# First loads of a channel-gating kernel as whole tiles on alternate queues, in place of halves on both

## The chip, the core and the metric

One core of a Trainium2 chip runs the kernel; the other seven do nothing of it. Names used below: TensorE does matmuls, VectorE sums and multiplies, ScalarE and SyncE mainly issue transfers here; 16 DMA engines move the data between the chip's main memory and SBUF, the memory on the core. A transfer has landed when the last of its completion updates has come in. The metric is the device time of one execution in microseconds (us), lower is better. Kernels are compared only within the same rounds. A ratio is the mean time of one kernel's fast runs over that of the other's of the same rounds, so it is not quite the ratio of the medians that are quoted; it comes with a 95% interval, and anything within 2% is called the same. A run over 1.5% above the fastest of its kernel counts as slow, and slow runs are not compared.

## The reference, cut to what matters

```python
x: (1, 384, 384, 384) bf16      # 113.25 MB
w1d: (1,) bf16                  # k = 1
g = mean of x over H and W      # one value per channel
s = sigmoid(g * w1d[0])
out = x * s                     # broadcast over H and W
```

Every output needs the mean of the whole input, so read literally x would be read twice. The kernel avoids that: it guesses the gate from the first four rows of each partition, gates and stores with that guess while it also sums everything, and at the end compares the true gate with the guess, bit by bit in bf16. If they differ, a second pass redoes all.

## The kernel before

x is seen as 1152 rows of 384 channels on each of 128 partitions: one first tile of 12 rows ("base"), and 19 tiles of 60 rows that go through 4 slots of SBUF. A row is 768 B per partition, a 60-row tile 46080 B per partition and 5.898 MB in all.

SyncE and ScalarE each issue DMAs into a queue of their own (in the profile q1 is SyncE's and q10 ScalarE's). The first loads (comments added, other lines cut):

```python
FIRST, EARLY, TILE, SLOTS, BOTH, FORE, OWN = 12, 4, 60, 4, 3, 32, 16
...
LEAD = EARLY + 4
load(base, FIRST, 0, hi=LEAD)                        # 8 of the 12 rows, SyncE
plan.dma("sync", w_one[0:1, 0:1], w1d.unsqueeze(0), writes=["w_one"])
for k in range(SLOTS):                               # slots 0, 1, 2 in halves, slot 3 whole
    load(slot(k), TILE, row0(k), ("sync", "scalar") if k < BOTH else ("sync",))
    if k == 0:
        load(base, FIRST, 0, ("scalar",), lo=LEAD)   # the other 4 rows, ScalarE
```

Then, for each tile, VectorE sums 16 of the 60 rows (`sum_own`, 10.5 us), TensorE sums the other 44 by matmuls with ones, VectorE multiplies the tile by the gate in place (`gate`, 12.1 us), ScalarE issues the store, and SyncE's load of the tile four later waits until that store has landed. A short ScalarE instruction delays load 4 once (comment added, the end of the loop cut):

```python
for k in range(n_tiles):
    if k >= SLOTS:
        for i in range(2) if k == SLOTS else () if k < SLOTS + 2 else (k - SLOTS,):
            sum_own(i)
            put(slot(i), TILE, row0(i), parts=None if i else (FORE, TILE - FORE))
        if k == SLOTS:
            pause(slot(k))     # ScalarE, 3.08 us; it waits for store 0 to land
        load(slot(k), TILE, row0(k), reads=["pause"] if k == SLOTS else ())
```

`put` is the gating and the issue of the store.

Of the kernel before, what the change touches and what calls it, by code (L numbers as in the profile page):

```python
# [149 lines left out]
def split(n, most):  # L150
    k = -(-n // most)
    return [n // k + (i < n % k) for i in range(k)]
# [3 lines left out]



FIRST, EARLY, TILE, SLOTS, BOTH, FORE, OWN = 12, 4, 60, 4, 3, 32, 16


PAUSE = 9
# [2 lines left out]
def bass_standalone__channel_attn_eca__vision_kernel(  # L165
# [5 lines left out]
    B, H, W, C = x.shape  # L171
    assert B == 1 and C == ROW and (B * H * W) % (4 * P) == 0
    n_rows = B * H * W // P
    x_rows, o_rows = x.flatten_outer_dims(), out.flatten_outer_dims()

    def dram(view, r0, n):
        return view[r0 * P : (r0 + n) * P, :].rearrange("(p t) c -> p (t c)", p=P)
# [21 lines left out]
    def at(r0, n):  # L199
        assert r0 + n <= n_arena  # L200
        return arena[:, r0 * C : (r0 + n) * C]

    def rows(r0, n):
        return [("sb", r) for r in range(r0, r0 + n)]
# [7 lines left out]
    base = SLOTS * TILE  # L212
# [5 lines left out]
    def slot(k):  # L218
        return k % SLOTS * TILE

    def row0(k):
        return FIRST + k * TILE
# [2 lines left out]
    s_true = at(base + FIRST, 1)  # L225
    plan = Planner(nc, "a", 70)

    def load(place, n, r0, queues=("sync",), lo=0, hi=None, reads=()):

        i, hi = lo, hi or n  # L230
        for queue, m in zip(queues, split(hi - lo, -(-(hi - lo) // len(queues)))):
            plan.dma(
                queue,
                at(place + i, m),
                dram(x_rows, r0, n)[:, i * C : (i + m) * C],
                reads=reads,
                writes=rows(place + i, m),
            )
            i += m

    loaded = []

# [40 lines left out]
    def sum_others():  # L283

        def one(e, s):
            e.wait_ge(ready, 1).then_inc(ready, -1)  # L286
            for r, n in ((0, FORE), (FORE, TILE - OWN - FORE)):
                add_rows(e, 1, (slot(s) + r) * C, n, False, False).then_inc(
                    plan.sems["tensor"], 1
                )  # L290

        def emit(e):
            add_rows(e, 1, (base + EARLY) * C, 4, True, False)
            rounds = -(-n_tiles // SLOTS)
            some = n_tiles - (rounds - 1) * SLOTS
            with e.Fori(0, rounds) as k:
                for s in range(some):
                    one(e, s)
                if some < SLOTS:
                    with e.If(k < rounds - 1):  # L300
                        for s in range(some, SLOTS):
                            one(e, s)
            add_rows(
                e, 1, (base + EARLY + 4) * C, FIRST - EARLY - 4, False, True
            ).then_inc(plan.sems["tensor"], 1)

        plan.streams["tensor"].append(("block", emit, None))
# [16 lines left out]
    def sum_own(k):  # L324

        r0 = slot(k) + TILE - OWN
        view = at(r0, OWN).rearrange("p (t c) -> p c t", t=OWN)
        to = part if k else own
        plan.op(
            "vector",  # L330
            lambda e: e.reduce_sum(to[:], view, axis=mybir.AxisListType.X),  # L331
            reads=rows(r0, OWN),
            writes=["part" if k else "own"],
        )
        if k:
            plan.op(
                "vector",
                lambda e: e.tensor_tensor(own[:], own[:], part[:], ALU.add),  # L338
                reads=["own", "part"],
                writes=["own"],  # L340
            )
# [37 lines left out]
    def put(place, n, r0, to=None, parts=None):  # L379
        to, i = place if to is None else to, 0  # L380
        for m in parts or [n]:
            plan.op(
                "vector",
                gate(to + i, place + i, m, s_early),
                reads=["s_early"] + rows(place + i, m),
                writes=rows(to + i, m),
            )
            i += m
        plan.final.append(
            plan.dma("scalar", dram(o_rows, r0, n), at(to, n), reads=rows(to, n))  # L390
        )

    def pause(r0):

        to = at(base + FIRST + 1, PAUSE)
        plan.op(
            "scalar",
            lambda e: e.activation(  # L398
                to, warm[:, 0:1].broadcast_to([P, PAUSE * C]), ACT_F.Sigmoid
            ),  # L400
            reads=["warm"],
            writes=rows(r0, 1) + ["pause"],
        )
# [26 lines left out]

    plan.op("gpsimd", lambda e: e.memset(warm[:, 0:1], 0.0), writes=["warm"])
    plan.op("vector", lambda e: e.memset(ones[:], 1.0), writes=["ones"])  # L432
    LEAD = EARLY + 4
    load(base, FIRST, 0, hi=LEAD)
    plan.dma("sync", w_one[0:1, 0:1], w1d.unsqueeze(0), writes=["w_one"])
    for k in range(SLOTS):
        load(slot(k), TILE, row0(k), ("sync", "scalar") if k < BOTH else ("sync",))
        if k == 0:
            load(base, FIRST, 0, ("scalar",), lo=LEAD)
    heads = {e: len(plan.streams[e]) for e in ("sync", "scalar")}  # L440
    weight()
    sum_first()
# [6 lines left out]
        reads=["total", "w_scaled0", "warm1"],  # L449
        writes=["s_early"],  # L450
    )
    plan.need("tensor", rows(base, LEAD))
    sum_others()

    for k in range(n_tiles):
# [5 lines that stand above are left out]
            if k == SLOTS:  # L461
                pause(slot(k))
            load(slot(k), TILE, row0(k), reads=["pause"] if k == SLOTS else ())
        there = rows(slot(k), TILE) + (rows(base + LEAD, FIRST - LEAD) if k == 1 else [])
        plan.relay(ready, "gpsimd", "tensor", there, rows(slot(k), FORE), ["acc1"])
        plan.signals("tensor", rows(slot(k) + FORE, TILE - OWN - FORE), ["acc1"])
    plan.signals("tensor", rows(base, FIRST), ["acc1"])
    for k in range(n_tiles - SLOTS, last):
# [15 lines left out]
        reads=["total", "w_scaled1"],  # L484
        writes=["s_true"],
# [6 lines left out]
        reads=["s_true", "s_early"],  # L492
        writes=["total"],
# [4 lines left out]
        reads=["total"],  # L498
        writes=["wrong"],
# [4 lines left out]
        reads=["wrong"],  # L504
        writes=["redo"],
# [5 lines left out]
    half, r0 = base // 2, 0  # L511
    for k, n in enumerate(split(n_rows, half)):
        place = k % 2 * half
# [4 lines left out]
            reads=rows(place, n),  # L518
            writes=rows(place, n),
# [98 lines left out]
```

## Time and profile before

| | before |
|---|---|
| time, median of 3 | 528.53 us (527.85 to 528.61) |
| bytes through the DMA engines | 226.5 MB, 430 GB/s over the span |
| VectorE busy | 451.1 us, 86% |
| TensorE busy | 178.2 us, 34% |
| 12-row tile: 8 rows landed / 4 rows landed | 7.7 / 22.4 us |
| slot 0 landed (first half / second half) | 18.5 / 14.5 us |
| store 0, 1, 2 issued | 38.6, 61.7, 84.7 us |
| store 0 landed, load 4 issued | 74.2, 77.3 us |

The timeline of VectorE before (start, length in us, engine, line, operation, operands; in brackets the idle time ahead of it and what ended it):

```profile
108.36 10.55 DVE L331 TENSOR_REDUCE part<-arena 128x384 f32<-128x6144 bf16 x1 [0.73 <-DMA arena<-in_x_dram]
135.47 10.54 DVE L331 TENSOR_REDUCE part<-arena 128x384 f32<-128x6144 bf16 x1 [3.90 <-DMA arena<-in_x_dram]
```

From 14.6 us on VectorE never waits for a load until tile 4, at 108 us; from tile 5 on it waits about 4 us for each. So VectorE has spare time in most of the run and none in the first 108 us.

### The profile page before, as it was taken

The page shows a single profiled execution, that of the slowest core. Times are in us where ns is not written, and L with a number is a line of the kernel's source. Part 1 is how long each engine was busy: PE and PEld are TensorE (multiplying, and loading weights), DVE is VectorE, ACT ScalarE, POOL GpSimd, SP SyncE. Part 2 cuts the span into 40 slices and gives each one's busy share as a digit, 9 for nine tenths or more (in the row PEclk, how much of TensorE's full clock was granted, in tenths as well). Part 3 has the DMA queues.
Part 4 walks back from the last instruction along what each step waited for, and adds up shares of the span by engine and source line. Part 5 has one row for each costly group of instructions (what it writes and reads, how often), then busy time and mean ns, then how long its engine had stood idle before and what let it go on. Part 6 is the DMA issues. An engine that isn't in the chain of part 4 may idle for free.

```text
span 526.7 us, 905 instructions
## 1 busy us (share of the span) xinstructions
PE 178.2 (34%) x640; PEld 0.2 (0%) x2; DVE 451.1 (86%) x82; ACT 5.8 (1%) x5; POOL 0.3 (0%) x5
## 2 busy tenths in 40 slices
PE   2534660060606051414233241515060606060701
PEld 0000000000000000000000000000000000000000
DVE  1899999999796969796969696979697979889796
ACT  1000020000000000000000000000000000000000
POOL 0000000000000000000000000000000000000000
PEclk9978877576766767675858585858585858576765
DMA  9999999999999999999999999999999999999998
GB/s 387 430 422 460 406 448 395 444 448 448 395 444 448 448 395 444 448 441 402 444 448 434 409 445 444 434 413 441 448 430 416 441 444 434 416 441 444 430 420 367
DMA packets 6340, 226.51 MB, mean 430 GB/s; under 512 B 706, under 2 KB 706, under 8 KB 962
## 3 DMA queue, kind: packets, MB, share of 16 engines
q10 hardware_dynamic: 3456, 122.49, 53.8%
q1 hardware_dynamic: 2882, 104.01, 45.9%
q14 instruction: 2, 0.02, 0.0%
HBM read 113.25 MB, written 113.25 MB: 430 GB/s over the span
## 4 chain that ended last, share of the span: by engine, by line
DMA 64%; DVE 27%; issue 4%; PE 2%; ACT 0%; DVEq 0%
DMA out_dram<-arena 33%; DMA arena<-in_x_dram 31%; DVE arena L209 13%; DVE part L331 12%; PE acc L247 1%; DVE own L338 1%; DVE total L319 0%; DVE own L356 0%; DVE terms L349 0%; ACT arena L481 0%; DVE total L489 0%; DVE total L374 0%; DVE wrong L497 0%; PE acc_own L247 0%; DVE redo L503 0%
## 5 line engine op out<-in xcount | busy, mean ns | idle before, releaser
L247 PE MATMUL acc<-arena,ones 128*128 128x512 bf16 x635 | 176.3, 447 | 314.0 <-PEq L286 314.0
L209 DVE TENSOR_TENSOR arena<-arena,s_early 128x23040 bf16<-128x23040 bf16 (+3 forms) x21 | 233.5, 11123 | 5.2 <-DMA arena<-in_x_dram 4.0
L331 DVE TENSOR_REDUCE part<-arena 128x384 f32<-128x6144 bf16 x18 | 189.5, 10526 | 53.4 <-DMA arena<-in_x_dram 53.4
L331 DVE TENSOR_REDUCE own<-arena 128x384 f32<-128x6144 bf16 x1 | 10.5, 10495 | 1.1 <-DMA arena<-in_x_dram 1.1
L338 DVE TENSOR_TENSOR own<-own,part 128x384 f32<-128x384 f32 x18 | 10.0, 558 | 0.6
L247 PE MATMUL acc_own<-terms,ones 128*128 128x384 bf16 x3 | 1.4, 478 | 16.8 <-DVE terms L349 16.8
L424 DVE TENSOR_SCALAR w_scaled<-w_all 128x1 f32<-128x1 f32 x2 | 0.2, 152 | 7.9 <-PE w_all L415 7.9
L481 ACT ACTIVATE arena<-total,w_scaled 128x384 bf16<-128x384 f32 x1 | 0.6, 614 | 444.3 <-DVE total L319 444.3
L319 DVE TENSOR_TENSOR total<-total,acc 128x128 f32<-128x128 f32 (+2 forms) x11 | 4.5, 408 | 0.4
L398 ACT ACTIVATE arena<-warm 128x3456 bf16<-128x3456 f32 x1 | 3.1, 3082 | 60.1 <-DMA out_dram<-arena 60.1
L415 PE MATMUL w_all<-w_one,ones 1*128 1x1 bf16 x1 | 0.2, 159 | 9.2 <-DMA w_one<-in_w1d_dram 9.2
L317 DVE COPY total<-acc 128x384 f32<-128x384 f32 x1 | 0.6, 558 | 1.2 <-PE acc L247 1.2
L409 ACT ACT_TABLE_LOAD x1 | 1.3, 1283 | 2.8 <-issue 2.8
L432 DVE MEMSET ones<- 128x128 bf16 x1 | 0.2, 165 | 1.3 <-PEq L603 1.3
L356 DVE TENSOR_TENSOR own<-own,terms 128x384 f32<-128x384 f32 x2 | 1.1, 559 | 0.1
L489 DVE TENSOR_TENSOR total<-arena,s_early 128x384 f32<-128x384 uint16 x1 | 0.6, 559 | 0.7 <-ACT arena L481 0.7
L349 DVE CAST terms<-own 128x384 bf16<-128x384 f32 x3 | 1.1, 357 | 0.1
L374 DVE TENSOR_TENSOR total<-total,acc_own 128x384 f32<-128x384 f32 x1 | 0.6, 556 | 0.6 <-PE acc_own L247 0.6
L446 ACT ACTIVATE s_early<-total,w_scaled 128x384 bf16<-128x384 f32 x1 | 0.6, 614 | 9.2 <-DVE total L319 9.2
L245 PE MATMUL acc<-arena,ones 128*128 128x512 bf16 x1 | 0.6, 608 | 0.0
L497 DVE TENSOR_REDUCE wrong<-total 128x1 f32<-128x384 f32 x1 | 0.6, 553 | 0.0
L409 ACT ACTIVATE warm<-warm 128x1 f32<-128x1 f32 x1 | 0.2, 202 | 0.0
(8 smaller groups left out, 0.9 us busy)
## 6 DMA issues: line engine op xcount, KB each, us to landing
out_dram<-arena ACTq DMA_DIRECT2D x19, 5760.0 KB, 44.7
arena<-in_x_dram SPq DMA_DIRECT2D x16, 5760.0 KB, 40.9
arena<-in_x_dram ACTq DMA_DIRECT2D x3, 2880.0 KB, 34.5
arena<-in_x_dram SPq DMA_DIRECT2D x3, 2880.0 KB, 29.0
out_dram<-arena ACTq DMA_DIRECT2D x1, 1152.0 KB, 11.1
arena<-in_x_dram SPq DMA_DIRECT2D x1, 768.0 KB, 7.7
arena<-in_x_dram ACTq DMA_DIRECT2D x1, 384.0 KB, 21.2
w_one<-in_w1d_dram SPq DMA_DIRECT2D x1, 0.0 KB
```

Source lines behind the costliest of these rows:

```text
L209: return lambda e: e.tensor_tensor(to_v, v, s_b, ALU.mult)
L245: loaded.append(e.matmul(bank, weights, moving, start=start, stop=stop))
L247: return e.add_instruction(mybir.InstMatmult(name=nc.get_next_instruction_name(), engine=mybir.EngineType.PE, ins=[e.lower_ap(moving), e.l ...
L317: emit = lambda e, part=part, of=of: e.tensor_copy(part, of)
L319: emit = lambda e, part=part, of=of: e.tensor_tensor(part, part, of, ALU.add)
L331: lambda e: e.reduce_sum(to[:], view, axis=mybir.AxisListType.X),
L338: lambda e: e.tensor_tensor(own[:], own[:], part[:], ALU.add),
L349: lambda e, term=term: e.tensor_copy(term, own[:]),
L356: lambda e, term=term: e.tensor_tensor(own[:], own[:], term, ALU.subtract),
L374: lambda e: e.tensor_tensor(total[:], total[:], acc_own[:, :C], ALU.add),
L398: lambda e: e.activation(to, warm[:, 0:1].broadcast_to([P, PAUSE * C]), ACT_F.Sigmoid),
L409: lambda e: e.activation(warm[:, 1:2], warm[:, 0:1], ACT_F.Sigmoid),
```

## The change

The intent is simpler loads: no tile is cut, both queues fed with long packets. SyncE's queue takes base, slot 1 and slot 3; ScalarE's takes slot 0 and slot 2.

```diff
-    LEAD = EARLY + 4
-    load(base, FIRST, 0, hi=LEAD)
+    load(base, FIRST, 0)
     plan.dma("sync", w_one[0:1, 0:1], w1d.unsqueeze(0), writes=["w_one"])
     for k in range(SLOTS):
-        load(slot(k), TILE, row0(k), ("sync", "scalar") if k < BOTH else ("sync",))
-        if k == 0:
-            load(base, FIRST, 0, ("scalar",), lo=LEAD)
+        load(slot(k), TILE, row0(k), "sync" if k % 2 else "scalar")
 ...
-    plan.need("tensor", rows(base, LEAD))
+    plan.need("tensor", rows(base, FIRST))
 ...
-        there = rows(slot(k), TILE) + (rows(base + LEAD, FIRST - LEAD) if k == 1 else [])
+        there = rows(slot(k), TILE)
```

(The body of `load`, which now issues one DMA, is cut.)

More of the change, by code (lines that the diff above doesn't have):

```diff
@@ L155 @@
 WIDE = 512
-FIRST, EARLY, TILE, SLOTS, BOTH, FORE, OWN = 12, 4, 60, 4, 3, 32, 16
+FIRST, EARLY, TILE, SLOTS, FORE, OWN = 12, 4, 60, 4, 32, 16
 PAUSE = 9
@@ L226, in bass_standalone__channel_attn_eca__vision_kernel, with load @@
     plan = Planner(nc, "a", 70)
-    def load(place, n, r0, queues=("sync",), lo=0, hi=None, reads=()):
-        i, hi = lo, hi or n
-        for queue, m in zip(queues, split(hi - lo, -(-(hi - lo) // len(queues)))):
-            plan.dma(
-                queue,
-                at(place + i, m),
-                dram(x_rows, r0, n)[:, i * C : (i + m) * C],
-                reads=reads,
-                writes=rows(place + i, m),
-            )
-            i += m
+    def load(place, n, r0, queue="sync", reads=()):
+        plan.dma(
+            queue, at(place, n), dram(x_rows, r0, n), reads=reads, writes=rows(place, n)
+        )
     loaded = []
```

## The prediction

> **What bounds the kernel now.** I read the page first (shares, slices, bytes), then a table of busy times by stage, then the issues and landings of single transfers, and last the first 110 us of the timeline. From the page:
>
> ```profile
> span 526.7 us, 905 instructions
> ...
> DMA  9999999999999999999999999999999999999998
> ...
> HBM read 113.25 MB, written 113.25 MB: 430 GB/s over the span
> ```
>
> The reader is to see that no slice has idle DMA engines: 226.5 MB go through them, and nothing in the change alters a byte of that. By stage (columns: stretch and length in us, busy us of PE, PEld, DVE, ACT, POOL, clock, DMA share, GB/s):
>
> ```profile
> 2.00:14.50 12.50, 2.83 (x7) 0.20 (x2) 2.76 (x8) 2.10 (x3) 0.00 (x0) 1.00 1.02 433
> 14.50:38.60 24.10, 11.83 (x39) 0.00 (x0) 22.79 (x4) 0.00 (x0) 0.00 (x0) 0.89 1.00 429
> 38.60:74.20 35.60, 19.32 (x69) 0.00 (x0) 35.53 (x6) 0.00 (x0) 0.00 (x0) 0.79 1.03 435
> 74.20:108.30 34.10, 5.70 (x26) 0.00 (x0) 33.39 (x4) 3.08 (x1) 0.00 (x0) 0.65 1.00 432
> 108.30:271.80 163.50, 54.41 (x198) 0.00 (x0) 139.07 (x18) 0.00 (x0) 0.00 (x0) 0.69 1.00 433
> 271.80:490.00 218.20, 72.80 (x264) 0.00 (x0) 185.45 (x25) 0.00 (x0) 0.00 (x0) 0.69 1.00 434
> ```
>
> From 2 us to 490 us the transfers run at 429 to 435 GB/s, whether only loads are under way (the first two rows) or loads and stores, and whether VectorE (DVE) is nearly always busy (the third and fourth rows) or 85% busy. So the DMA engines are the bound, VectorE is close behind only up to 108 us, and at 433 GB/s the 226.5 MB alone take 523 us of the 526.7. All that a change of queues could save is the rest, about 4 us or 0.7%; what it could cost is any stretch in which both queues are empty.
>
> **What the Trainium skill says.** "DMA: Bandwidth & Descriptors", Specifications, gives a fabric ceiling of 435 GB/s; the trace agrees (432 to 434 in the long stages). The same page, "Issuing engines are not separate DMA queues", says that the queues of SyncE and ScalarE run on the same 16 engines, and that a second issuer saves only issue time. The trace agrees in the last stage: the stores that ScalarE alone has in flight land at 496.7, 510.3 and 523.9 us (issue plus issue-to-landing of each), 5.898 MB every 13.6 us, 434 GB/s from one queue. Its section "Queues, rings and completion order" says that each engine round-robins between its queues packet by packet. That matters here, because a queue with short packets then gets a small share of the bytes. The DMA view of the stretch from 14.5 to 22.4 us, when ScalarE's queue holds the last four rows of the first tile (3072 B on each partition) and SyncE's holds half tiles (23040 B):
>
> ```profile
> DMA packets 289, 3.41 MB, mean 431 GB/s; under 512 B 32, under 2 KB 32, under 8 KB 158
> ...
> q1 hardware_dynamic: 143, 2.93, 86.1%
> q10 hardware_dynamic: 146, 0.48, 14.9%
> ```
>
> Equal packets (143 and 146), bytes of 6 to 1. So a packet is one partition's run, and each engine has 8 of them per transfer. At 433/16 = 27.1 GB/s per engine one takes 0.23 us (8 rows), 0.34 us (12 rows), 0.85 us (30 rows), 1.70 us (60 rows). The check: 8 rounds of 0.85 + 0.11 us are 7.7 us, and those four rows landed at 22.4 us, 7.9 us after the transfer ahead of them (14.5).
>
> **The change, part by part.** (1) It removes four of eight first loads and their issues: 3 halves and the four-row piece. An issue costs its sequencer 0.33 to 0.66 us, beside transfers that are queued for 50 us; gain none. (2) It makes packets of 60 rows where halves had 30. Both ran at full rate above; gain none. (3) It changes the order of arrival, which is the real part. Before, from the timeline:
>
> ```profile
> 9.18 0.16 PE L415 MATMUL w_all<-w_one,ones 1*128 1x1 bf16 x1 [9.18 <-DMA w_one<-in_w1d_dram]
> 13.51 0.61 ACT L446 ACTIVATE s_early<-total,w_scaled 128x384 bf16<-128x384 f32 x1 [9.19 <-DVE total L319]
> 14.56 10.49 DVE L331 TENSOR_REDUCE own<-arena 128x384 f32<-128x6144 bf16 x1 [1.08 <-DMA arena<-in_x_dram]
> 26.31 12.23 DVE L209 TENSOR_TENSOR arena<-arena,s_early 128x12288 bf16<-128x12288 bf16 x2 [1.26 <-PE acc L247]
> 38.57 0.36 ACTq L109 DMA_DIRECT2D out_dram<-arena  x1
> ```
>
> VectorE sums its 16 rows when ScalarE's half of slot 0 has landed (14.5), gates from 26.3 (TensorE has summed the rows by then), and the first store is issued at 38.57.
>
> After, worked out from the packet times. SyncE's packets flow from 1.05 us, ScalarE's only from about 2.9 (no packet of its queue starts before 2.6 in this trace); by then about 3.75 of the 8 packets of the 12-row tile are through. The other 4.25 each alternate with a 60-row packet: 4.25 x (1.70 + 0.34) = 8.7, so the tile **lands at about 11.6** (before: 7.7 for the 8 rows), the weight one packet later, at 13.3, and the early gate vector is ready 5.0 us after it, as before (9.15 to 14.1): **18.3**. Slot 0 has 3.75 packets left at 11.6, each paired with one of slot 1: 3.75 x 3.4 = 12.8, so **slot 0 lands at about 24.4**, 10 us later than its second half did and 6 later than its first. (Bytes: 1.18 + 5.90 + 2.76 = 9.84 MB at 433 GB/s are 22.7 us, from about 1.8: the same.) The gate vector is ready before that and not on the path.
>
> Then VectorE: 10.5 us of summing to 34.9 (TensorE's 7.65 us beside it), 12.2 of gating: **store 0 is issued at 47.2**, 8.6 later than before. One tile costs VectorE 10.5 + 0.56 + 12.1 = 23.15 us, so stores 1, 2 and 3 follow at 70.3, 93.5 and 116.6 (before: 61.7, 84.7, 107.7). Slot 1 lands at 24.4 + 4.25 x 3.4 = 39, slot 2 at 24.4 + 8 x 3.4 = 51.6, both ahead of VectorE.
>
> **What of this reaches the end.** ScalarE's queue is in order: a store goes out only when the loads before it have. Before, slot 2's second half leaves that queue by 50 to 53 us (issued at 2.29, landed at 53.2), so store 0, issued at 38.57, only waited in it, and landed at 74.2. After, slot 2 leaves it at about 51, still later than 47.2. All first loads and store 0 are 30.7 MB either way, so store 0 lands at 74 either way, the 3.08 us pause follows, and load 4 is issued at 77.3 either way. What is lost is slack of VectorE: store 1 must be in the queue when store 0's last packets leave, 72 to 73.8 (before 61.7, after 70.3: 2 to 3 us to spare); store 2 when store 1 ends, 94.1 (before 84.7, after 93.5: nearly nothing, but SyncE's queue then holds load 4 and fills the engines); store 3 by 121.3 (116.6). Before, VectorE waited some 4 us per tile for loads from 108 us on, 27.3 per tile against its 23.15; so the 9 us are caught up by about tile 6, at 163 us, and the rest of the run is the same. Sum: 0 us, minus perhaps 0.3 for fewer small packets at the start, plus a hole if store 1 comes late.
>
> **Rivals.** (a) *Earlier start wins*: whole tiles cut overheads and the kernel gets faster. For: eight rows of 6 KB packets at the start. Against: the rate is already 433 from 2 us on; at most 0.3 us. (b) *Late VectorE opens a hole*: both queues empty between store 0 and store 1, because SyncE's queue is dry from slot 3's landing (70.8 before) until load 4, issued at 77.3, gets its first packet. For: only 2 to 3 us of slack, and the landings of one transfer on 16 engines are spread by 2 to 4 us at this stage. Each us of delay beyond would be a us at the end: 530 to 533. Chance about one in six. (c) *A shifted phase between loads and stores*: if store 2 finds its queue empty, loads run ahead by one or two packets, 2 to 3 us; the pause of 3.08 us shows that somebody tuned this phase. Against: at the end the last gating ends at 502.1, and the store before it lands only at 510.3, so there are 8 us to spare. Worth within 1 us.
>
> **Range and chances.** Most likely nothing: 528.5, the median before. Below, the start gives 0.3 and the runs' own spread 0.7, so 526.8; above, the hole of (b) up to 3 us: 531.2. 2% is 10.6 us; a gain of that size is more than the DMA floor allows, a loss would need a hole five times the one I can see.
>
> **What would show it.** In the changed kernel: the 12-row tile landing at 11 to 13, the sum of VectorE's own rows starting at 23 to 26 (wrong if at 30: then queues share bytes, not packets), store 0 issued at 46 to 49 and store 1 at 69 to 72, pause at 74, load 4 issued at 77, VectorE's first wait for a load at tile 5 or 6 rather than 4, DMA rate unchanged in every stage. The prediction is wrong if slot 0 lands so late that store 1 misses 73.8, seen as a slice of low GB/s near 75 us, or if the later phase of loads and stores lowers the rate below 430.

## The result, and the profile after

The changed kernel took **528.64 us** in the median (528.16 to 530.8, 6 runs) against 528.5 before (527.85 to 528.94, 6 runs); ratio 1.0015, interval 0.9994 to 1.0037: the same. Timed again later (five runs): 530.73 against 528.23, ratio 1.0043 (1.0030 to 1.0057), so still the same by the 2% rule, but there it is a little slower. That 2 us is taken up below.

From the page after:

```profile
span 527.1 us, 890 instructions
...
DMA  9999999999999999999999999999999999999998
...
HBM read 113.25 MB, written 113.25 MB: 430 GB/s over the span
```

The stages after, cut at the same times as those before (same columns):

```profile
38.60:74.20 35.60, 18.75 (x71) 0.00 (x0) 35.30 (x6) 0.00 (x0) 0.00 (x0) 0.74 1.01 423
74.20:108.30 34.10, 7.02 (x27) 0.00 (x0) 34.03 (x6) 3.08 (x1) 0.00 (x0) 0.60 1.01 435
108.30:271.80 163.50, 59.51 (x195) 0.00 (x0) 145.57 (x19) 0.00 (x0) 0.00 (x0) 0.63 1.00 433
271.80:490.00 218.20, 79.97 (x260) 0.00 (x0) 185.42 (x24) 0.00 (x0) 0.00 (x0) 0.63 1.00 433
```

The last two columns are what counts: the DMA share stays at 1.0 in every stage, and from 74 us on the rate is that of before to within 3 GB/s. The 423 in the first row (435 before) is no idle time, its share is 1.01. In part it is bookkeeping, since a packet's bytes are booked where it starts; spread over the packets' durations the two rates are 419 and 423. Both lie under 433 because one load packet on each engine takes longer than 1.70 us about when ScalarE's queue passes from its last load to the first store: 1.9 to 3.1 us at 47 to 49 us here, 2.2 to 2.75 at 49 to 53 before. That is 1.2 us per engine here against 0.8 before. VectorE's work has moved: busy 145.6 us between 108 and 272 us instead of 139.1, because it still catches up there.

```profile
18.57 0.16 PE L407 MATMUL w_all<-w_one,ones 1*128 1x1 bf16 x1 [18.57 <-DMA w_one<-in_w1d_dram]
...
22.78 10.56 DVE L323 TENSOR_REDUCE own<-arena 128x384 f32<-128x6144 bf16 x1
...
33.25 12.22 DVE L209 TENSOR_TENSOR arena<-arena,s_early 128x12288 bf16<-128x12288 bf16 x2
45.51 23.86 ACTq L109 DMA_DIRECT2D out_dram<-arena  x2
...
163.07 10.55 DVE L323 TENSOR_REDUCE part<-arena 128x384 f32<-128x6144 bf16 x1 [1.83 <-DMA arena<-in_x_dram]
```

These are the timeline's answers to the rows of before: the weight arrives 9.4 us later (9.18 to 18.57), VectorE's sum starts 8.2 us later (14.56 to 22.78), the gating 6.9 us later, store 0 is issued 6.9 us later, and VectorE's first longer wait for a load comes at tile 6, at 163 us, instead of at tile 4 (it also waited 0.26 us for slot 1, at 45.7). Store 0 landed at 74.7 us (74.2 before), and load 4 was issued at 77.8 (77.3 before). So store 0 is issued seven us late and lands half a us late, about what the longer packets above cost.

### The profile page after: what moved, and what is told of

The parts are those of the page before. It is cut to its first block, busy times and chain, and to the rows that moved or that the text cites. A ratio compares the mean times of both kernels' runs of the same rounds, so it can differ in the third digit from the quotient of the medians.

```text
span 527.1 us, 890 instructions
## 1 busy us (share of the span) xinstructions
PE 187.6 (36%) x630; PEld 0.2 (0%) x2; DVE 450.9 (86%) x82; ACT 5.8 (1%) x5; POOL 0.3 (0%) x5
## 3 DMA queue, kind: packets, MB, share of 16 engines
q1 hardware_dynamic: 2594, 101.45, 44.8%
## 4 chain that ended last, share of the span: by engine, by line
DMA 71%; DVE 26%; issue 2%; ACT 0%; PE 0%
DMA arena<-in_x_dram 38%; DMA out_dram<-arena 32%; DVE part L323 12%; DVE arena L209 12%; DVE own L330 1%; DVE total L311 0%; DVE own L348 0%; DVE terms L341 0%; ACT arena L470 0%; DVE total L478 0%; DVE total L366 0%; DVE wrong L486 0%; PE acc_own L239 0%; DVE redo L492 0%
## 5 line engine op out<-in xcount | busy, mean ns | idle before, releaser
L239 PE MATMUL acc<-arena,ones 128*128 128x512 bf16 x625 | 185.7, 467 | 296.6 <-PEq L278 295.4
L237 PE MATMUL acc<-arena,ones 128*128 128x512 bf16 x1 | 0.6, 609 | 0.0
## 6 DMA issues: line engine op xcount, KB each, us to landing
arena<-in_x_dram SPq DMA_DIRECT2D x1, 1152.0 KB, 15.6
out_dram<-arena ACTq DMA_DIRECT2D x1, 1152.0 KB, 11.1
```

The lines of the kernel that those rows point to most:

```text
L237: loaded.append(e.matmul(bank, weights, moving, start=start, stop=stop))
L239: return e.add_instruction(mybir.InstMatmult(name=nc.get_next_instruction_name(), engine=mybir.EngineType.PE, ins=[e.lower_ap(moving), e.l ...
```

## The experiments

Twelve runs followed, in three groups of four on three chips (3, 6 and 4), each group with the kernel before timed beside it. The first four delay VectorE ahead of the first gating by a dummy sum, in order to find how much lateness is free; the next four take the change apart; the last four test an explanation of the 2 us, which falls. All gave the right result.

### How much lateness is free

```diff
+                if i == 0:      # rows summed again: 8, 16 or 16 + 16
+                    plan.op("vector", reduce_sum(part, <rows of slot 0>), ...)
                 put(slot(i), TILE, row0(i), ...)
```

Changed kernel, 8 rows (5.3 us):

> The changed kernel with one extra VectorE sum of 8 rows (about 5.3 us, half of the 10.5 us of 16 rows) ahead of the first gating. Theory (the DMA engines are the bound; only a stretch with both queues empty costs time): store 1 is issued at 69.0 + 5.3 = 74.3 us, its first packets at about 75.5, while store 0's last packets end at about 73.9: a hole of 1.5 to 2.5 us, time 530 to 531. Rival (the first store is on the path): all 5.3 us reach the end, 534. Rival (queue order does not matter at all, slack is larger): 528.6.

Changed kernel, 16 rows (10.5 us):

> The same with 16 extra rows, 10.5 us. Theory: store 1 is issued at 79.6 us; the hole from 73.9 us is ended by load 4, issued at 77.8 behind the pause, first packets about 79: a hole of some 5 us, time 533.5. Rival (the first store is on the path): 539. Rival (more slack than I see): 528.6.

Kernel before, 16 rows:

> The kernel before with 10.5 us more of VectorE ahead of the first gating. Theory: store 1 moves from 61.7 to 72.2 us, still just ahead of the end of store 0 (73.8): no hole or under 0.5 us, time 528.5 to 529. Rival (the first store is on the path): 539. It also copies the changed kernel's late start of stores without any change of the loads.

Kernel before, 32 rows (21 us):

> The kernel before with 21 us more of VectorE ahead of the first gating. Theory: store 1 at 82.8 us, the hole from 73.8 ended by load 4 (issued at 77.3, first packets about 78.6): 5 us, time 533.5, although the delay is 21 us. Rival (the first store is on the path): 549.

| kernel | store 1 issued | DMA engines idle between 70 and 85 us | median, us | ratio to before (interval) |
|---|---|---|---|---|
| before | 61.7 | 0 | 528.95 in this group | 1 |
| after | 69.0 | 0 | 528.64, again 530.73 | 1.0015, again 1.0043 |
| before + 10.5 us | 70.6 | 0 | 530.25 | 1.0018 (0.9993 to 1.0043) |
| after + 5.3 us | 74.3 | 1.2 us | 535.86 | 1.0119 (1.0088 to 1.0149) |
| after + 10.5 us | 79.0 | 6.6 us | 539.06 | 1.0223 (1.0171 to 1.0274), unclear at 2% |
| before + 21 us | 81.4 | 8.8 us | 543.41 | 1.0257 (1.0222 to 1.0292), slower |

(The idle column is worked out from the start and duration of every packet in the trace, over the 16 engines. A stretch in which both queues are empty is called a hole.) Store 0's packets end at 72.8 to 74.4 us, engine by engine, in all of them. A store 1 issued up to 70.6 us opens no hole; one issued at 74.3 does. The DMA engines from 70 to 84 us (share and GB/s in the last columns), first in "before + 10.5 us", then in the changed kernel:

```profile
70.00:84.00 14.00, 7.92 (x32) 0.00 (x0) 13.97 (x4) 3.08 (x1) 0.00 (x0) 0.87 1.06 458
...
70.00:84.00 14.00, 9.81 (x33) 0.00 (x0) 13.96 (x3) 3.08 (x1) 0.00 (x0) 0.74 1.01 438
```

The kernel before with its stores 9 us late is as fast as the changed kernel: within the noise (the interval reaches 0.4%) the lateness that the change brings is free, whichever way it is brought about. The rival "the first store is on the path" would have made it 539. For "after + 10.5 us" the same rival also said 539, and 539.06 was measured. The number alone would mislead there; the trace shows engines idle for 6.6 us, and the rival misses the same delay in the kernel before by 9 us and the delay of 21 us by 6 (549 against 543.41).

My sizes were wrong, though. The hole of the last row was to be ended at about 79 us by load 4. The timeline of that run, around the hole:

```profile
81.28 10.42 DVE L331 TENSOR_REDUCE part<-arena 128x384 f32<-128x6144 bf16 x1
81.40 0.35 ACTq L109 DMA_DIRECT2D out_dram<-arena  x1
81.79 3.08 ACT L398 ACTIVATE arena<-warm 128x3456 bf16<-128x3456 f32 x1 [67.52 <-DVE arena L209]
84.90 0.33 SPq L109 DMA_DIRECT2D arena<-in_x_dram  x1
```

and its DMA engines from 70 to 84 us (share and GB/s in the last columns):

```profile
70.00:84.00 14.00, 0.00 (x0) 0.00 (x0) 14.00 (x2) 2.21 (x1) 0.00 (x0) 0.64 0.39 168
```

The pause stands behind store 1 in ScalarE's instruction stream. While ScalarE waits for VectorE to be done with slot 1, the pause cannot run, and so SyncE's load 4 cannot be issued, though store 0 landed at 74. A late store 1 empties **both** queues, and the hole ends only with store 1 itself, whose first packet starts at 82.3. In all three runs with a hole that first packet starts 0.86 us after the issue.

The holes alone also do not make up the times: 1.2 us of hole came with 6.9 us more time (535.86 against 528.95), 8.8 with 14.5. The two traces say where the rest lies. In "after + 5.3 us" the last DMA engine ends 8.2 us later than in the profile of the kernel before: 1.2 of them are idle time, 3.2 are longer packets (an engine's packets add up to 528.6 us in the mean, against 525.4), and 3.8 come from the last engine being further behind the mean of the 16. In "before + 21 us" the 16.5 us are 8.8, 4.4 and 3.3. So the engines also end further apart after a hole, 5.6 us from first to last in both traces against 1.5 before. Why packets are longer after a hole is not shown.

### The change taken apart

Slot 0 in four transfers of 15 rows on the same queue, everything else as in the changed kernel (the edit shortened):

```diff
-        load(slot(0), TILE, row0(0), "scalar")
+        for i in range(0, TILE, 15):
+            plan.dma("scalar", at(slot(0) + i, 15), <rows i to i + 15 of tile 0>, ...)
```

> The changed kernel with slot 0 loaded as four transfers of 15 rows on the same queue, so packets of 11520 B instead of 46080 B; no byte and no queue changes. Theory (the engines alternate packet by packet, whatever their size): the 12-row tile lands at about 7.6 us instead of 15.6 (5 rounds of 0.43 + 0.34 us and a turn for the completion write, from 2.9), but slot 0 then gets 0.43 us of every 2.13 against slot 1's and slot 3's 60-row packets and lands at about 47 us instead of 22.4; store 0 at about 70; ScalarE's queue dry from about 60 to 71, and again from about 84 to 89: time 540 to 545. Rival (queues share by bytes, or in order of issue): the tile at 15.6, slot 0 at 22 to 24, time 528.6.

Measured: 552.01 against 528.23 us, ratio 1.0464 (1.0445 to 1.0483). The landing of the 12-row tile in the changed kernel (from the issues in the first 0.05 us; count, size, us to landing):

```profile
arena<-in_x_dram SPq DMA_DIRECT2D x1, 1152.0 KB, 15.6
```

and in this one:

```profile
arena<-in_x_dram SPq DMA_DIRECT2D x1, 1152.0 KB, 7.8
```

The last piece of slot 0 landed at 46.4 us instead of 22.4. Both are within 0.6 us of what packet-by-packet turns give (7.6 and 47), and far from the rival's 15.6 and 22 to 24. The price is seen in two holes (both rows by the same columns as before):

```profile
60.00:70.00 10.00, 9.95 (x47) 0.00 (x0) 10.00 (x3) 0.00 (x0) 0.00 (x0) 1.00 0.00 0
...
84.00:94.00 10.00, 0.00 (x0) 0.00 (x0) 10.00 (x2) 1.22 (x1) 0.00 (x0) 0.50 0.17 74
```

10.8 and 9.5 us idle, 20.3 of the 23.8 us lost. I had put the second at 5, again because load 4 was not behind store 1 in my account. So packet size, with no byte more, is worth 24 us here (the cut also adds three completion writes on each engine): the loads of one queue starve when their packets are short beside the other queue's long ones.

The 12-row tile whole, the slots still in halves (the waits for its rows change as in the diff above):

```diff
-    load(base, FIRST, 0, hi=LEAD)
+    load(base, FIRST, 0)
-        if k == 0:
-            load(base, FIRST, 0, ("scalar",), lo=LEAD)
```

> One part of the change alone: the 12-row tile whole on SyncE's queue, the slots still in halves. Theory: the tile lands at about 10 us (5 rounds of 0.85 + 0.34 us and a turn for the completion write, from 2.9), the early gate vector at 17, store 0 at 40 to 43, store 1 at 64 to 67: no hole, time 528.5 within 0.7. Rival (each part has a cost that the other hides): off by over 1.5 us.

The tile landed at 10.2 us and no hole opened, as expected (stores 0 and 1 came at 44.8 and 68.0, 1 to 2 us later than I had put them), but the times did not hold: 527.88, 530.86 and 532.7 us, and a fourth of 537.51 that counts as slow. The ratio, 1.0103 (1.0056 to 1.0150), comes out only with that slow run in it: the three runs that were not profiled average 533.69 us. The two fast ones of them average 531.78 us, 0.7% above the 528.23 of the kernel before. The one profiled run is the one of 527.88, so what made the others slow is not in a trace.

Slots whole, the 12-row tile still in 8 and 4 rows:

```diff
-        load(slot(k), TILE, row0(k), ("sync", "scalar") if k < BOTH else ("sync",))
+        load(slot(k), TILE, row0(k), ("sync",) if k % 2 else ("scalar",))
```

> The other part alone: slots whole on alternate queues, the 12-row tile still in 8 rows on SyncE's queue and 4 on ScalarE's behind slot 0. Theory: the 8 rows land at about 12.5 us, slot 0 at about 23.5, the 4 rows only at about 40 (8 packets and a completion write, each behind a 60-row packet of 1.7 us), slot 2 at about 60, so store 0, issued at 46, starts at 60 but still lands at 74, since no byte is added: no hole, time 528.5 within 0.7. Rival (a late store 0 costs what it is late): several us slower.

528.57 us, ratio 1.0004 (0.9989 to 1.0019). The 8 rows landed at 11.1 us, slot 0 at 24.7 (both within 1.5 us of the theory), the 4 rows at 39.3 us, slot 2 at 60.7, store 0 at 74.4. Store 0 was issued at 47.4 and had to wait 13 us in ScalarE's queue behind slot 2: nothing of that reaches the end, since the engines carried other bytes meanwhile.

The changed kernel itself again, for its two runs near 530.7:

> The changed kernel itself, to see whether its two runs near 530.7 us come again. Theory: 528.6 in most runs; if 530.7 returns in a share of them, something in the start is near an edge (the slack of store 1, 4.9 us in the profiled run, or the phase of loads and stores), and the kernel before, timed beside it, shows none.

530.73 us (530.27 to 531.66) against 528.23 (528.02 to 528.48, nine runs in the same rounds): every run of the changed kernel was slower than every one of the kernel before. No hole before 520 us. What differs is the very end. Last stretches of the kernel before (DMA share and GB/s in the last columns):

```profile
524.00:525.00 1.00, 0.00 (x0) 0.00 (x0) 0.00 (x0) 0.00 (x0) 0.00 (x0) 0.50 0.91 387
525.00:526.00 1.00, 0.00 (x0) 0.00 (x0) 0.00 (x0) 0.00 (x0) 0.00 (x0) 0.50 0.18 74
526.00:527.00 1.00, 0.00 (x0) 0.00 (x0) 0.00 (x0) 0.00 (x0) 0.00 (x0) 0.50 0.02 8
```

and of the changed kernel in this run:

```profile
526.00:527.00 1.00, 0.00 (x0) 0.00 (x0) 0.93 (x3) 0.00 (x0) 0.00 (x0) 0.50 0.11 46
527.00:528.00 1.00, 0.00 (x0) 0.00 (x0) 0.08 (x1) 0.00 (x0) 0.00 (x0) 0.50 0.15 65
528.00:529.00 1.00, 0.00 (x0) 0.00 (x0) 0.00 (x0) 0.00 (x0) 0.00 (x0) 0.50 0.13 55
529.00:530.00 1.00, 0.00 (x0) 0.00 (x0) 0.00 (x0) 0.00 (x0) 0.00 (x0) 0.50 0.07 27
```

A share of 0.07 to 0.15 is one or two of the 16 engines (1/16 = 0.06). The completion updates of the last store say the same: the first engine is done at 526.0 us, thirteen by 526.9, the last two only at 529.6 and 530.1.

### An explanation of the last engine, and how it fell

In `after_again` the 16 engines' parts of load 4 land 2.3 us apart, before they do so 0.6 us apart. Store 2 is issued at 92.4 us there, just as store 1 runs out (landed 94.9). My theory: where a queue has just run dry, an engine takes two packets of the other queue in a row and falls out of step by one packet (1.7 us), and engines out of step get slower. Tests: take the pause away, so that store 1 ends later and store 2 is in time; or make only store 2 late in the kernel before (a dummy sum of 12 rows ahead of its gating).

```diff
-            if k == SLOTS:
-                pause(slot(k))
-            load(slot(k), TILE, row0(k), reads=["pause"] if k == SLOTS else ())
+            load(slot(k), TILE, row0(k))
```

> The changed kernel without the 3.08 us pause ahead of load 4. New theory: the changed kernel loses nothing in holes, but store 2, issued at 92.1 to 92.4 us, just misses the end of store 1 (its last packets start at 90.5 to 91.5): on some engines two load packets follow each other, the engines fall one packet (1.7 us) out of step with each other, load packets then take longer now and then, and the last engine ends 2 to 4 us after the first. Without the pause load 4 shares the engines with store 1 earlier, store 1 ends at 96 to 97, store 2 comes in time: the spread of one landing over the 16 engines stays under 1 us from 95 us on, ratio to the kernel before 0.998 to 1.001. Rival (whole first tiles themselves put the engines out of step): spread 2 us as with the pause, ratio 1.002 to 1.005.

> The kernel before with 7.9 us (a sum of 12 rows) more of VectorE ahead of the gating of slot 2 only; loads, store 0 and store 1 stay. Store 2 is issued at 92.6 us instead of 84.7. New theory: the spread at the landing of load 4 goes from 0.6 to over 1.7 us and stays, ratio 1.002 to 1.006. Rival (the order or size of the first loads does it): spread 0.6, ratio 0.999 to 1.001.

> Control: the kernel before without the pause. New theory: store 2 has 10 us of slack with and without it; spread under 1 us, ratio 0.998 to 1.002. Rival (the phase of loads against stores that the pause sets is what counts): off by over 0.5%.

> The 12-row tile whole, the slots in halves, without the pause. With the pause this kernel's store 2 came at 91.1 us, at the very edge, and its times lay between 527.9 and 537.5. New theory: away from the edge the scatter goes: all within 1 us of the kernel before. Rival (its scatter has another cause): runs over 530 us again.

| profiled run | its time, us | load 4: spread over the engines | end: first engine, last engine, spread |
|---|---|---|---|
| before | 528.24 | 0.6 | 525.2, 526.7, 1.5 |
| after_no_pause | 528.37 | 1.9 | 525.4, 526.8, 1.4 |
| base_whole_slots_halved | 527.88 | 0.6 | 524.8, 526.3, 1.5 |
| base_split_slots_whole | 528.51 | 2.5 | 525.5, 526.9, 1.5 |
| after | 528.60 | 2.1 | 525.4, 527.1, 1.7 |
| before_store2_late | 529.25 | 2.7 | 525.3, 527.7, 2.4 |
| before_delay10 | 530.88 | 2.3 | 526.5, 529.3, 2.9 |
| after_again | 531.66 | 2.3 | 526.0, 530.1, 4.1 |
| halved_no_pause | 531.66 | 3.1 | 525.3, 530.1, 4.8 |
| before_no_pause | 533.40 | 0.7 | 525.2, 531.8, 6.6 |

(Spread: last minus first of the 16 completion updates of a transfer in the trace. The rows come from different groups and chips, one trace each.) Half of the theory holds: a late store 2 does put the engines out of step (0.6 to 2.7 us, with the loads of before). But it is not the only way into it: without the pause store 2 of the changed kernel and of `halved_no_pause` was issued in time, at 91.9 us with store 1 landing at 98, and the spread at load 4 was still 1.9 and 3.1 us, not under 1. And being out of step costs nothing by itself: `before_store2_late` took 528.38 us in the median, ratio 0.9984 (0.9963 to 1.0004). And the control, in step at load 4 (0.7 us), ended worst: ratio 1.0050 (1.0019 to 1.0080), right at the limit of 0.5% that was set for the rival about the pause, with one or two engines at work from 526 us on:

```profile
528.00:529.00 1.00, 0.00 (x0) 0.00 (x0) 0.00 (x0) 0.00 (x0) 0.00 (x0) 0.50 0.04 17
529.00:530.00 1.00, 0.00 (x0) 0.00 (x0) 0.00 (x0) 0.00 (x0) 0.00 (x0) 0.50 0.07 28
530.00:531.00 1.00, 0.00 (x0) 0.00 (x0) 0.00 (x0) 0.00 (x0) 0.00 (x0) 0.50 0.07 28
```

`after_no_pause` gave 1.0016 (0.9997 to 1.0035), no cure; `halved_no_pause` scattered again, 528.07 to 533.41 us, ratio 1.0025 (0.9997 to 1.0054). The theory that the edge at store 2 costs the 2 us has fallen.

What the table does show: in these runs without a hole the first engine to finish does so at 524.8 to 526.5 us, and the spread to the last one, 1.4 to 6.6 us, carries most of the difference in time. A 60-row load packet takes 1.70 us at its quickest and 1.709 us in the mean before, 1.720 in `after_again`. Why some packets are slow, and on which engine, stays open, and so does the part of the change in it. The kernel before shows such times too (its own runs beside the last four experiments, on chip 4, went from 528.3 to 531.0). But on chip 6 it stayed within 528.5 while all five runs of the changed kernel took 530.3 or more. In those same rounds whole slots alone lost nothing (528.57) and the whole 12-row tile alone did (530.86 and 532.7 of its fast runs), which points to that tile. It is a lead and not shown: `before_no_pause` doesn't have that tile and was slower still.

No version beat the kernel before. With the first engine done at 525.2 and the DMA engines full from 2 us on, only the spread at the end and the first 1 to 2 us are left.

## Why the prediction was right, point by point

The time was right for the reason given: the DMA engines are full, and lateness of VectorE counts only where both queues run dry. Store 1 had about 4 us to spare (69.0 against about 73) where 2 to 3 were predicted, so the errors at the start, told below, did not reach the end.

- **The bound.** Right: DMA share 1.0 and 433 GB/s in the long stages before and after, time the same.
- **Fewer and longer transfers gain nothing.** Right, for the whole tiles alone too (ratio 1.0004). (Four of nine first loads went, not of eight.)
- **Landing of the 12-row tile, "about 11.6".** Wrong by 4.0: it landed at 15.6. Two terms were mis-sized. By the time ScalarE's packets flow (2.6 to 3.3 us) 3 of its 8 packets were through, not 3.75, so 5 rounds of 2.05 us follow instead of 4.25: +1.5. And the completion write is a packet that takes a turn of its own: the tile's last data packets start at 12.5 to 13.2 us, its 4-byte completion packets at 14.6 to 15.3, after one more 60-row packet: +1.7. The rest is the late start of ScalarE's first packets on some engines (3.3 us, not 2.9) and 0.3 from the last completion packet to the landing. The prediction's check, 7.7 us worked out against 7.9 measured, agreed by luck: it left out the completion turn of the four rows, and just there SyncE's queue had completion packets too, at 17.6 to 18.0 us, so that this turn cost next to nothing. The "under 512 B 32" of the view shown are these 2 x 16 packets. The weight, a two-byte transfer behind it, needed two more turns and landed at 18.4 instead of 13.3; the gate vector was ready at 23.5 instead of 18.3.
- **Slot 0, "about 24.4".** It landed at 22.4, 2 us sooner for the same reason: turns that SyncE spent on short and tiny packets went to slot 0. So the gate vector came 1 us after slot 0 and not 6 before; VectorE's sum started at 22.78 and not at 22.44, because VectorE was busy with its part of the gate vector until then (to 22.86). So "not on the path" was wrong, by 0.3 us.
- **Slot 1, "39".** It landed at 45.7: the same two terms passed on, and the weight's two turns; VectorE waited 0.26 us for it. That margin I had put at 8 us.
- **Stores.** Store 0 at 45.5 (47.2 predicted), then 69.0, 92.1 and 115.1 (70.3, 93.5, 116.6): each 1.3 to 1.7 sooner, in step with slot 0. Of the signs named, the sum (23 to 26) and store 0 (46 to 49) so came just too early, and the 12-row tile (11 to 13) too late.
- **Nothing passes 74 us.** Right: store 0 landed at 74.7, load 4 was issued at 77.8. The free lateness was confirmed on the kernel before (store 1 at 70.6, no hole), and its end on the changed one (store 1 at 74.3, a hole).
- **Caught up by tile 6, at 163 us.** Right to the us: first wait at 163.07.
- **Rival (b), the hole.** The condition was right, its size was not: I let load 4 end it, but load 4 stands behind the pause and the pause behind store 1 on ScalarE. Nothing bounds that hole but store 1.
- **Rival (c), the phase.** "Worth within 1 us" was too little: two of the six first runs, and all five of the later ones, were some 2 us slower (through the last engine, in the one of them that was profiled), and the pause, which I took for a sign of tuning, is worth 0.5% in the kernel before (1.0050 without it). The runs don't show why, nor that the 2 us are a matter of this phase.

## What to carry to other kernels

When the DMA engines are full from start to end, rearranged loads move only slack: work out which queue could run dry first and when, and compare that with the lateness you bring, here 69.0 us against about 73 (store 0's packets end at about 74, and a store issued into empty queues took 0.86 us to its first packet). Two queues share the engines by packets and not by bytes (the same 12-row tile landed at 7.8, 10.2 or 15.6 us by the other queue's packets), so a tile that is wanted early should not go in short packets beside long ones. And look through the instruction order of the issuing engine, since a wait ahead of an unrelated issue can empty both queues at once.

## What the Trainium skill lacked or had wrong

- "DMA: Bandwidth & Descriptors", Queues, rings and completion order: it states the turns between queues at packet granularity, which all runs here agree with, but not what follows for shares. It has a packet as some 9 to 17 descriptors; in the profile's packets the turn passed after one partition's run, up to 46080 B for 1.70 us (143 packets of one queue and 146 of the other between 14.5 and 22.4 us of the kernel before); the same 12-row tile took 15.6 us to land beside 46080 B packets, 10.2 beside 23040 B and 7.8 beside 11520 B.
- The same section doesn't say that a completion write waits for a turn like a data packet: 1.7 us behind a 60-row packet here, and two such turns for the two-byte weight.
- No page looked up for this has the delay of a transfer that enters a dry queue while the other is busy: load 4 of the kernel before was issued at 77.34 us and its first packet started at 81.88, against 1.0 us for the first load of the run and 0.86 for a store into two empty queues. In the fourteen traces load 4 took 3.9 to 5.0 us to its first packet.
- "Perfetto Trace Analysis", What "DMA-bound" means, names single DMA engines as a possible bound. These runs agree, and add a size: without any idle stretch, the last of 16 engines ended 1.4 to 6.6 us after the first.
